# x tile 3 loaded and turned earlier, and filler matmuls on the built-in ones constant, in a fused attention and MLP kernel

## The chip, the cores and the metric

The kernel runs on one core of a Trainium2 chip. The metric is device microseconds of one execution. "Span" is the stretch from the first to the last instruction of a profiled execution; it is about 1.2 us shorter than the time. In the text PE is TensorE, SP the engine that issues most DMAs, and a "turn" is a DMA (DMA_TRANSPOSE in the profile) that writes a 128-row tile transposed. The mean granted clock that the profiles show is 1.00.

## The reference

```
x: [1, 2048, 640] bf16, wqkv [640, 1920], 32 heads of 20
g   = sigmoid(sum(x * gate_w))
q, k, v = split(x @ wqkv);  phi(t) = where(t > 0, t + 1, exp(t)) + 1e-6
a   = linear attention of phi(q), phi(k), v over all tokens, @ wo
x1  = x + shift(gelu(layernorm(x) @ w1)) @ w2
b   = x1 + gelu(layernorm(x1) @ w3) @ w4
out = g * a + (1 - g) * b
```

What matters here is the very start: q and k need x with its features on the partitions, that is, x turned, for all 16 tiles of 128 tokens.

## The kernel before

A small scheduling layer records every operation, works out the waits, and picks the PE order with a time model at build time. The DMA queue of SP carries, in program order, the loads and the turns. PE turns tiles 0 to 2 itself, with a VectorE copy out of PSUM; SP turns tiles 3 to 15.

```python
dma_in(x_tok[:, 0, :], ...); dma_in(x_tok[:, 1, :], ...)      # x tiles 0, 1
load_wq(0)
dma_in(x_tok[:, 2, :], x2[256:384, :], "x2")
for k in range(1, KD):
    load_wq(k)                                                # query weights, 5 slices
for k in range(KD):                                           # key weights, 5 slices
    dma_in(wkg[:, k, 0:D], A_wqkv[128 * k:128 * (k + 1), D:2 * D], "wk%d" % k)
    if k == 2:
        dma_in(x_tok[:, 3, :], x2[384:512, :], "x3")
# ... (gate weight, on the ACT queue)
for c in range(1, NCH):                                       # tiles 4-7, 8-11, 12-15
    dma_in(x_tok[:, 4 * c:4 * c + 4, :], x2[512 * c:512 * (c + 1), :]..., "xc%d" % c)
    for t in range(3 if c == 1 else 4 * c, 4 * c + 4):
        sch.dma("sp", xT[:, :, 128 * t:128 * (t + 1)], x_tok[:, t, :], "trx%d" % (t % 4), transpose=True)
# ...
memset(pool, xn[:, 0, 0:128], 1.0)                            # what the fillers multiply
WARM = 3200; WARM2 = 256
# PE: filler of WARM columns, turn tiles 0 and 1, filler of WARM2, then queries of
# tiles 0-2 slice by slice (with a filler of 256 and the turn of tile 2 in between),
# keys of tiles 0-2, then for t = 3 .. 15: query tile t, key tile t
```

Fillers are matmuls whose result nobody reads. They keep PE busy until data comes.

Of the kernel before, what the change touches and what calls it, by code (L numbers as in the profile page):

```python
# [5 lines left out]
BF16 = mybir.dt.bfloat16  # L6
# [410 lines left out]
def _build(nc, A_x, A_wqkv, A_wo, B_w1, B_w2, B_w3, B_w4, gate_w, out, dbg=None, stop=None):  # L417
    sch = _Sched(nc)
# [41 lines left out]
    ps = nc.alloc_psum_tensor("ps", [128, 8, 512], F32)  # L460
# [18 lines left out]
    x_tok = pa.alloc("x_tok", [128, NT, D], BF16)  # L479
# [9 lines left out]
    xn = pa.alloc("xn", [128, 3, D], BF16)  # L489
# [4 lines left out]
    xT = ra.alloc("xT", [128, KD, S], BF16)  # L494
# [19 lines left out]
    def bank():  # L514
        best = None
        for k_ in range(nbanks[0]):
            b = (bank_rr[0] + k_) % nbanks[0]
            if b in bank_pend or b in bank_hold:
                continue
            lk = sch.locks.get(b)  # L520
            tfree = 0.0 if lk is None else sch.ev_time.get((lk[1].sem, lk[1].val), 1e18)
            if best is None or tfree < best[0]:
                best = (tfree, b)
        bank_rr[0] = best[1] + 1
        bank_pend.add(best[1])
        return best[1]
# [46 lines left out]
    def dve(fn, reads, writes, cost=None):  # L573
        if cost is None:
            n = nfree(writes[0])
            cost = 65.0 + n / 0.96
        return sch.op("dve", fn, reads, writes, cost=cost)
# [7 lines left out]
    def pe(fn, reads, writes, cost=500.0):  # L585
        for w_ in writes:
            sp_, rl = sch.rects(w_)
            if sp_ == "ps":
                for (_p0, _p1, lo, hi) in rl:
                    for b in range(lo // PS_BANK, (hi - 1) // PS_BANK + 1):  # L590
                        bank_pend.discard(b)
        return sch.op("pe", fn, reads, writes, cost=cost)
# [65 lines left out]
    def memset(engf, ap, val):  # L658
        return engf(lambda e: e.memset(ap, val), [], [ap])  # L659
# [13 lines left out]
    def dma_in(out_ap, in_ap, key, **kw):  # L673
        return sch.dma("sp", out_ap, in_ap, key, **kw)
# [11 lines left out]
        load_wq(k)  # L686
    for k in range(KD):
        dma_in(wkg[:, k, 0:D], A_wqkv[128 * k:128 * (k + 1), D:2 * D], "wk%d" % k)
        if k == 2:
            dma_in(x_tok[:, 3, :], x2[384:512, :], "x3")  # L690
    gwr = xn[:, 1, 0:128]
    dve(lambda e: e.memset(gwr, 0.0), [], [gwr])
    sch.dma("act", xn[0:KD, 1, 0:128], gate_w.rearrange("(k p) -> k p", p=128), "gw")
    for c in range(1, NCH):
        dma_in(x_tok[:, 4 * c:4 * c + 4, :], x2[512 * c:512 * (c + 1), :].rearrange("(n p) d -> p n d", p=128), "xc%d" % c)
        for t in range(3 if c == 1 else 4 * c, 4 * c + 4):
            sch.dma("sp", xT[:, :, 128 * t:128 * (t + 1)], x_tok[:, t, :], "trx%d" % (t % 4), transpose=True)

    k_done = {}

# [26 lines left out]
                        wo_rows(h, e, ns), "wo", group_total=5, deps=dp)  # L727
        sch.dma("pool", wo_aug[64:104, 4, :], A_wo[600:D, :], "wo", group_total=5, deps=dp)

    memset(pool, xn[:, 0, 0:128], 1.0)  # L730
    memset(pool, ones_c[:], 1.0)
    memset(pool, wkg[:, :, D:D + 1], 1.0)
    aselect(ident[:], ones_c[:, 0:128], [[-1, 128]], ALU.is_equal, 0, 1)
# [18 lines left out]

    IT = _Items()
    WARM = 3200
    WARM2 = 256

    def t_x(t):
        b = bank()
        tr_group(b, [x_tok[:, t, 128 * k:128 * (k + 1)] for k in range(KD)])
        src = psb(b, 0, D).rearrange("p (k c) -> p k c", k=KD)  # L760
        dst = xT[:, :, 128 * t:128 * (t + 1)]
        if t == 2:
            mm_group(ps[:, b, 448:448 + KD], [(gwr, ident[:, 0:KD])])
        copy(dve, dst, src)
        if t == 2:
            copy(dve, wkg[:, :, D + 1:D + 2], ps[:, b, 448:448 + KD].rearrange("p (k o) -> p k o", o=1))
# [80 lines left out]

    def warmup(cols, cyc):
        b = bank()
        steps = [512] * (cols // 512) + [128] * (cols % 512 // 128)  # L850

        def fn(e):
            ins = None
            for n in steps:
                ins = e.matmul(ps[:, b, 0:n], xn[:, 0, 0:128], xn[:, 0, 0:128].unsqueeze(1).to_broadcast([128, n // 128, 128]), start=True, stop=True)  # L855
            return ins
        pe(fn, [xn[:, 0, 0:128]], [ps[:, b, :]], cost=cols * cyc)

    def q_tile(t):
        tok = slice(128 * t, 128 * (t + 1))  # L860
# [5 lines left out]
    def stream(order, w, n2, done):  # L866
        bs = {}
        for t, k in order:
            if k is None:
                if t is None:  # L870
                    warmup(256, 0.42)
                else:
                    t_x(t)
                continue
            if k == 0:
                bs[t] = pair()
                bank_hold.update((bs[t], bs[t] + 1))
            b = bs[t]
            l = xT[:, k, 128 * t:128 * (t + 1)]

            def fn(e, l=l, b=b, k=k):
                e.matmul(ps[:, b, 0:512], l, w[:, k, 0:512], start=(k == 0), stop=(k == KD - 1))  # L882
                return e.matmul(ps[:, b + 1, 0:n2], l, w[:, k, 512:512 + n2], start=(k == 0), stop=(k == KD - 1))  # L883
            pe(fn, [w[:, k, 0:512 + n2], l], [ps[:, b, 0:512], ps[:, b + 1, 0:n2]], cost=272.0)
            if k == KD - 1:
                bank_hold.difference_update((b, b + 1))
                done(t, b)
# [13 lines left out]
    def addA(name, dur, fn, deps=()):  # L901
        IT.add("A", name, dur, fn, deps)

    addA(("warm",), 0.0, lambda: warmup(WARM, 0.834))
    for i in range(2):
        addA(("tx", i), 0.28, lambda i=i: t_x(i))
    addA(("warm", 1), 0.0, lambda: warmup(WARM2, 0.42))
    addA(("q", 2), 4.08, q_three)
    addA(("k", 1), 2.72, k_two)
# [288 lines left out]
    for t in range(NT):  # L1198
        c = t // 4
# [53 lines left out]
    for t in range(NT):  # L1253
        c = t // 4
# [30 lines left out]
def bass_gated_mix__linear_attn_block__mixer_s_mlp__prompt_kernel(  # L1285
    nc, A_x, A_wqkv, A_wo, B_x, B_w1, B_w2, B_w3, B_w4, gate_w, out
):
    assert tuple(A_x.shape) == (1, S, D) and tuple(out.shape) == (1, S, D)
    assert tuple(A_wqkv.shape) == (D, 3 * D) and tuple(A_wo.shape) == (D, D)
    assert tuple(B_w1.shape) == (D, D) and tuple(B_w2.shape) == (D, D)  # L1290
    assert tuple(B_w3.shape) == (D, F) and tuple(B_w4.shape) == (F, D) and tuple(gate_w.shape) == (D,)
    _build(nc, A_x, A_wqkv, A_wo, B_w1, B_w2, B_w3, B_w4, gate_w, out)
# [28 lines left out]
```

## Time and profile before

| kernel before | us |
|---|---|
| time, median of 3 runs (range) | 260.52 (260.36 to 261.09) |
| span of the profile | 259.8 |
| PE busy | 254.8, 98% of the span |
| first filler matmul starts | 1.05 |
| first query matmul starts | 5.11 |
| query matmul of tile 4, first weight load | 17.50 |

The page of the kernel before: its busy line (engine, us, share, instructions) and the first lines of the chain of work that ended last.

```profile
PE 254.8 (98%) x1655; PEld 133.0 (51%) x1686; DVE 152.0 (59%) x288; ACT 106.5 (41%) x216; POOL 93.6 (36%) x152
...
PE 98%; issue 1%; DVE 0%; POOL 0%; POOLq 0%
```

The whole execution hangs on PE, and PE is never idle for long. So a change of DMA order can gain only where PE waits or works slowly, and that is the start.

The timeline of PE of the kernel before (start us, us, engine, line, operation, tiles, count, and in brackets the idle time before and what ended it):

```profile
1.05 2.85 PE L855 MATMUL ps<-xn 128*128 128x512 bf16 x7 [1.05 <-POOL xn L659]
...
5.11 0.59 PE L882 MATMUL ps<-wq,xT 128*128 128x512 bf16 x1
...
6.95 0.38 PE L882 MATMUL ps<-wq,xT 128*128 128x512 bf16 x1
```

And its weight loads (PEld), around the moment when the array becomes fast, and at tile 4:

```profile
6.88 0.15 PEld L882 LDWEIGHTS ps<-wq,xT 128*128 128x128 bf16 x1
6.95 0.10 PEld L883 LDWEIGHTS ps<-wq,xT 128*128 128x128 bf16 x1
...
17.50 0.10 PEld L600 LDWEIGHTS ps<-wq,xT 128*128 128x128 bf16 x1
```

The fillers wait for a memset of POOL. A weight load takes 0.15 us until 6.88 and 0.10 us from 6.95 on (two loads just after a pause of PE, at 5.08 and 5.11, took 0.10 as well). The 512-column matmuls go from 0.63 to 0.38 us at the same place. That is the speed-up of the array, called "the clock" from here on (a name only); weight loads show it best, because they all have one shape. (The granted clock of the profile reads 1.00 in the slow stretch too; it does not show this.)

SP's timeline of the kernel before, the loads and turns of x (the load that was issued at 7.41 has tiles 4 to 7):

```profile
5.98 0.43 SPq L285 DMA_DIRECT2D x_tok<-in_A_x_dram  x1
...
7.41 0.43 SPq L285 DMA_DIRECT2D x_tok<-in_A_x_dram  x1
...
9.85 1.29 SPq L281 DMA_TRANSPOSE xT<-x_tok  x1
13.54 5.89 SPq L281 DMA_TRANSPOSE xT<-x_tok  x4
19.47 0.58 SPq L285 DMA_DIRECT2D x_tok<-in_A_x_dram  x1
```

A turn that waits for its load is issued as soon as the load has landed: the last landing marks of tile 3 and of tiles 4 to 7 stand at 9.84 and 13.52, the turns at 9.85 and 13.54. When a turned tile has landed is read from its completion marks in the trace, of which there are 16, as many as the DMA engines that the page counts (that each engine sets one is my reading, not shown); the last one counts.

### The profile page before, as it was taken

The numbers are of one execution on the slowest core, as the hardware profiler recorded it, in microseconds if no ns is written. First come the engines' busy times: TensorE is split into PE (matmuls) and PEld (weight loads), VectorE is DVE, ScalarE is ACT, GpSimd is POOL, SyncE is SP. The second block draws the span as 40 slices with busy tenths as digits, with TensorE's granted clock in tenths as the row PEclk, the third lists the DMA queues.
The fourth block names the chain that finished last, engine by engine and source line by source line (L and its number), as shares of the span: only waits on it lengthen the run. The fifth ranks groups of instructions, "written<-read, shape, count | busy, mean of one in ns | idle before, by whom it ended". The sixth has DMA issues, their size and how long they took to land.

```text
span 259.8 us, 4263 instructions
## 1 busy us (share of the span) xinstructions
PE 254.8 (98%) x1655; PEld 133.0 (51%) x1686; DVE 152.0 (59%) x288; ACT 106.5 (41%) x216; POOL 93.6 (36%) x152
## 2 busy tenths in 40 slices
PE   8999999999999999999999999999999999999996
PEld 4555555554445455555444545554455544455453
DVE  1487787899912799999998407993033410143233
ACT  1396767751355766685854140005500045200000
POOL 4003996869963019667904202230011110021001
DMA  6955886581756991552726650132000020000211
GB/s 185 288 86 150 175 207 154 166 140 39 110 113 124 360 327 32 76 101 52 104 46 122 124 73 0 39 83 82 0 3 0 3 101 0 0 3 1 103 50 50
DMA packets 51390, 25.16 MB, mean 97 GB/s; under 512 B 42750, under 2 KB 49959, under 8 KB 51370
## 3 DMA queue, kind: packets, MB, share of 16 engines
q1 hardware_dynamic: 49984, 21.47, 36.0%
q0 software_dynamic: 1136, 3.28, 5.1%
q8 instruction: 13, 0.21, 0.4%
q10 hardware_dynamic: 250, 0.14, 0.2%
q14 instruction: 7, 0.06, 0.1%
HBM read 12.05 MB, written 2.62 MB: 56 GB/s over the span
## 4 chain that ended last, share of the span: by engine, by line
PE 98%; issue 1%; DVE 0%; POOL 0%; POOLq 0%
PE ps L600 61%; PE ps L1160 21%; PE ps L790 8%; PE ps L882 2%; PE ps L855 1%; PE ps L1072 1%; PE ps L1142 1%; PE ps L883 1%; PE ps L611 1%; DVE x_tok L639 0%; PE ps L962 0%; PE ps L991 0%; PE ps L1139 0%; POOL xn L659 0%; POOLq L1306 0%
## 5 line engine op out<-in xcount | busy, mean ns | idle before, releaser
L600 PE MATMUL ps<-xnT,w 128*128 128x512 bf16 x348 | 80.4, 379 | 0.7 <-issue 0.2
L1160 PE MATMUL ps<-w,h2T 128*128 128x512 bf16 (+1 forms) x409 | 58.3, 298 | 0.5 <-issue 0.2
L656 ACT ACTIVATE h2T<-ps 128x512 bf16<-128x512 f32 x52 | 30.5, 598 | 67.6 <-PE ps L600 67.5
L600 PEld LDWEIGHTS ps<-xnT,w 128*128 128x128 bf16 x360 | 34.2, 98 | 38.5 <-issue 0.9
L639 DVE SCALAR_TENSOR_TENSOR x_tok<-ps,stg,abx 128x512 bf16<-128x512 f32 (+1 forms) x32 | 17.3, 550 | 61.5 <-PE ps L1160 61.5
L622 POOL TENSOR_SCALAR abx<-x_tok,stg 128x640 f32<-128x640 bf16 x16 | 15.3, 956 | 99.1 <-DVE x_tok L639 94.9
L1160 PEld LDWEIGHTS ps<-w,h2T 128*128 128x128 bf16 x416 | 32.1, 98 | 24.9 <-issue 1.1
L622 POOL TENSOR_SCALAR xn<-x_tok,st 128x640 bf16<-128x640 bf16 x32 | 34.9, 1099 | 13.8 <-DMA xnT<-xn 13.3
L656 ACT ACTIVATE Er<-ps 128x640 bf16<-128x640 f32 x32 | 22.4, 708 | 17.7 <-PE ps L600 7.9
L655 ACT ACTIVATE junk<-x_tok 128x640 bf16<-128x640 bf16 x32 | 23.7, 739 | 3.1 <-DVE x_tok L637 2.6
L656 ACT ACTIVATE hsT<-ps 128x512 bf16<-128x512 f32 (+1 forms) x32 | 18.9, 593 | 13.1 <-PE ps L600 12.7
L600 PE MATMUL ps<-M_sb,pqnT 128*128 128x128 bf16 (+1 forms) x156 | 23.6, 297 | 0.3
L600 PE MATMUL ps<-w,hsT 128*128 128x512 bf16 (+1 forms) x160 | 23.7, 299 | 0.0
L639 DVE SCALAR_TENSOR_TENSOR abx<-ps,stg,abx 128x640 f32<-128x640 f32 x16 | 14.1, 883 | 12.6 <-PE ps L600 11.6
L600 PE MATMUL ps<-wkg,xT 128*128 128x130 bf16 (+1 forms) x138 | 21.1, 298 | 0.1
L600 PE MATMUL ps<-wq,xT 128*128 128x128 bf16 (+1 forms) x128 | 19.7, 298 | 0.1
L600 PEld LDWEIGHTS ps<-w,hsT 128*128 128x128 bf16 x160 | 13.3, 98 | 12.1
L600 PEld LDWEIGHTS ps<-M_sb,pqnT 128*128 128x128 bf16 x160 | 13.2, 98 | 10.8
L790 PE MATMUL ps<-pk_tok,x_tok 128*128 128x512 bf16 x79 | 17.7, 379 | 0.1
L622 DVE TENSOR_SCALAR Er<-Er 128x640 bf16<-128x640 bf16 x32 | 11.6, 361 | 9.6 <-ACT Er L656 9.3
L1101 DVE TENSOR_TENSOR pq_tok<-pq_tok,dnr 128x300 bf16<-128x300 bf16 (+1 forms) x48 | 16.8, 403 | 0.6
L637 DVE SCALAR_TENSOR_TENSOR x_tok<-ps,x_tok 128x640 bf16<-128x640 f32 x16 | 13.1, 820 | 6.5 <-PE ps L600 5.9
(79 smaller groups left out, 229.1 us busy)
## 6 DMA issues: line engine op xcount, KB each, us to landing
w<-in_B_w_dram SPq DMA_DIRECT2D x1, 2160.0 KB, 9.7
w<-in_B_w_dram SPq DMA_DIRECT2D x1, 2080.0 KB, 15.2
x_tok<-in_A_x_dram SPq DMA_DIRECT2D x3, 640.0 KB, 5.5
out_dram<-x_tok SPq DMA_DIRECT2D x3, 640.0 KB, 3.1
w<-in_B_w_dram POOLq DMA_DIRECT2D x8, 160.0 KB, 3.7
wq<-in_A_wqkv_dram SPq DMA_DIRECT2D x5, 160.0 KB, 3.2
wkg<-in_A_wqkv_dram SPq DMA_DIRECT2D x5, 160.0 KB, 3.9
wv<-in_A_wqkv_dram POOLq DMA_DIRECT2D x1, 800.0 KB, 5.5
```

The source lines that it names most:

```text
L600: ins = e.matmul(out_ap, l, r, start=(i == 0), stop=(i == n - 1))
L611: ins = e.transpose(o, s_, ident[:])
L622: return engf(lambda e: e.tensor_scalar(out_ap, in_ap, s1, s2, op0, op1), rd, [out_ap], cost=cost)
L637: return dve(lambda e: e.scalar_tensor_tensor(out_ap, in0, scalar, in1, op0, op1, accum_out=accum), rd, [out_ap, accum], cost=cost + 70.0)
L639: return dve(lambda e: e.scalar_tensor_tensor(out_ap, in0, scalar, in1, op0, op1), rd, [out_ap], cost=cost)
L655: return act(lambda e: e.activation(out_ap, in_ap, func, bias=bias, scale=scale, accum_out=accum), rd, wr, cost=cost)
L656: return act(lambda e: e.activation(out_ap, in_ap, func, bias=bias, scale=scale), rd, wr, cost=cost)
L790: ins = e.matmul(o, l, r, start=(t0 + q_ == 0), stop=(t0 + q_ == NT - 1))
L855: ins = e.matmul(ps[:, b, 0:n], xn[:, 0, 0:128], xn[:, 0, 0:128].unsqueeze(1).to_broadcast([128, n // 128, 128]), start=True, stop=True)
L882: e.matmul(ps[:, b, 0:512], l, w[:, k, 0:512], start=(k == 0), stop=(k == KD - 1))
L1101: dve(lambda e, o=o, i0=i0, i1=i1: e.tensor_tensor(o, i0, i1, ALU.mult), [i0, dnr[:, 1, sd, :]], [o], cost=cost)
L1160: ins = e.matmul(o, l, r, start=False, stop=(i == KFF - 1), skip_group_check=(n0 > 0))
```

## The change

The intent: get tile 3 turned sooner, by loading it behind the first key slice and issuing its turn ahead of the load of tiles 4 to 7; and start the fillers sooner, by letting them read a constant that the program's preamble has made, in place of a tile that POOL must fill first. The second filler is doubled, which fills what the earlier start frees.

```diff
     for k in range(KD):
         dma_in(wkg[:, k, 0:D], ..., "wk%d" % k)
-        if k == 2:
+        if k == 0:
             dma_in(x_tok[:, 3, :], x2[384:512, :], "x3")
+    def x_turn(t): ...            # the turn of tile t, as before
+    x_turn(3)
     ...
     for c in range(1, NCH):
         dma_in(x_tok[:, 4 * c:4 * c + 4, :], ..., "xc%d" % c)
-        for t in range(3 if c == 1 else 4 * c, 4 * c + 4):
-            sch.dma("sp", xT[...], x_tok[:, t, :], ..., transpose=True)
+        for t in range(4 * c, 4 * c + 4):
+            x_turn(t)
...
-    memset(pool, xn[:, 0, 0:128], 1.0)
-    WARM2 = 256
+    WARM2 = 512
...
+        one = nc.const_aps.tensor(1.0, [128, 512], BF16)
-                ins = e.matmul(ps[:, b, 0:n], xn[:, 0, 0:128], xn[:, 0, 0:128]... repeated, ...)
+                ins = e.matmul(ps[:, b, 0:n], one[:, 0:128], one[:, 0:n], ...)
```

More of the change, by code (lines that the diff above doesn't have):

```diff
@@ L688, in _build, with x_turn @@
         dma_in(wkg[:, k, 0:D], A_wqkv[128 * k:128 * (k + 1), D:2 * D], "wk%d" % k)
-        if k == 2:
+        if k == 0:
             dma_in(x_tok[:, 3, :], x2[384:512, :], "x3")
+    def x_turn(t):
+        sch.dma("sp", xT[:, :, 128 * t:128 * (t + 1)], x_tok[:, t, :], "trx%d" % (t % 4), transpose=True)
+    x_turn(3)
     gwr = xn[:, 1, 0:128]
@@ L695, in _build @@
         dma_in(x_tok[:, 4 * c:4 * c + 4, :], x2[512 * c:512 * (c + 1), :].rearrange("(n p) d -> p n d", p=128), "xc%d" % c)
-        for t in range(3 if c == 1 else 4 * c, 4 * c + 4):
-            sch.dma("sp", xT[:, :, 128 * t:128 * (t + 1)], x_tok[:, t, :], "trx%d" % (t % 4), transpose=True)
+        for t in range(4 * c, 4 * c + 4):
+            x_turn(t)
     k_done = {}
@@ L854, in fn @@
             for n in steps:
-                ins = e.matmul(ps[:, b, 0:n], xn[:, 0, 0:128], xn[:, 0, 0:128].unsqueeze(1).to_broadcast([128, n // 128, 128]), start=True, stop=True)
+                ins = e.matmul(ps[:, b, 0:n], one[:, 0:128], one[:, 0:n], start=True, stop=True)
             return ins
-        pe(fn, [xn[:, 0, 0:128]], [ps[:, b, :]], cost=cols * cyc)
+        pe(fn, [], [ps[:, b, :]], cost=cols * cyc)
     def q_tile(t):
```

## The prediction

> **What bounds the kernel.** The page's busy table has PE at 254.8 us, 98% of the 259.8 us span, and the chain of waits that ended last is PE for 98%. From 13.61 us on the chain has no PE pause over 0.1 us until the tail at 257, so only the first 13.6 us hold anything to win. There (timeline of PE and weight loads) fillers run from 1.05 to about 3.7, the transposes of tiles 0 and 1 to 4.8, two 128-column fillers, then real work from 5.11. The array is slow at first (427 ns per 512 columns in the fillers; 216 ns from 6.95 on). It speeds up between 6.24 and 6.95.
>
> **Fillers.** The first filler waits for the memset of its tile (POOL, 0.79 + 0.20); the built-in ones exist at 0.37, so it can start about 0.2 us earlier, at 0.85. Tile 0 of x lands at 3.29 and tile 1 at 3.62 (landing stamps of the trace), so the transposes can move up by 0.2 us too. The second filler doubles to 512 columns: +0.21 us at the slow clock. Net, the first query matmul (5.11) moves by -0.1 to 0 us. More gain needs the fast clock to come sooner. [...] At best (fast at 5.1) the 1.8 us of slow work shrinks by 0.9 us.
>
> **Tile 3.** Before, x tile 3 was issued at 5.98, landed at 9.84, was turned from 9.85 and the turned tile landed at 14.27, just behind the load of tiles 4-7 (issued 7.41, landed 13.52). It is needed at 14.81: PE did not wait. The change issues it at 5.04, so it should land near 9.0 and be turned by about 12: more slack, nothing gained. The cost follows on the same queue: SP waits for tile 3 (9.0), issues the turn (1.29 us), and only then, at about 10.3 instead of 7.41, issues the load of tiles 4-7. The queue moves 300 GB/s until 12, so the old early issue mostly waited in line; the next chunk, alone, took 4.4 us (19.47 to 23.86). I estimate landing at 14.2 to 15.0, 1 us later than before. Tile 4's turn took 3.9 us before, tile 8's 2.4 us; tile 4 thus lands at 16.8 to 18.8 and is needed at 17.5 (before: 17.45). I expect a PE wait of 0 to 1.2 us before the query matmul of tile 4, mean 0.3. Tiles 5 to 15 keep slack.
>
> **Sum.** About -0.2 (start, clock) + 0.3 (tile 4) - 0.2 for a PE order, chosen by the builder's model, that may shift slightly: nearly nothing. I predict 260.4 us, 8 in 10 between 259.6 and 261.4. Faster by over 2%: 0.01; within 2%: 0.97; slower: 0.02.
>
> **What would show it.** First filler at 0.85; first query matmul at 5.0 to 5.1; the speed-up at 6.2 to 6.9 as before (or earlier: then up to -0.9 us); tile 3's turned landing near 12; the load of tiles 4-7 issued near 10.3; a PE wait on the turn of tile 4 near 17.5; after 20 us only a constant shift.
>
> **What would make it wrong.** [...] the turn of tile 4 taking 4 us again, so that PE loses over 1 us; a builder order that differs in the later stages and leaves gaps.

The sum came to -0.1 us: -0.2, +0.3 and -0.2, from the 260.52 us measured before to 260.4. The start alone was worth -0.1 to 0 us, and the rest of the -0.2 is estimate, not shown.

## The result

| | before | changed |
|---|---|---|
| time, median of 6 runs, us | 260.88 | 261.01 |
| range, us | 260.36 to 261.12 | 260.71 to 261.43 |
| span of the profile, us | 259.81 | 259.76 |

The ratio is 1.0009, with a 95% interval of 0.9995 to 1.0022. A ratio is the mean time of one kernel's fast runs over the mean of the other's fast runs of the same rounds, so it is not quite the ratio of the medians. Nothing that these runs can show has changed. (The median of before went from 260.52 to 260.88 with three more runs: a few tenths of a microsecond is the noise of these numbers.)

The changed kernel's page, the busy line and the chain:

```profile
PE 256.8 (99%) x1685; PEld 133.0 (51%) x1685; DVE 152.4 (59%) x288; ACT 106.6 (41%) x216; POOL 94.2 (36%) x151
...
PE 98%; DVE 1%; issue 0%
```

(The 2 us more of PE busy are matmul records that were missing in the other trace, 1685 against 1655; they aren't work.) Its PE timeline:

```profile
0.83 2.83 PE L860 MATMUL ps<-const-bfloat16-1.0 128*128 128x512 bf16 x7 [0.83 <-PEq L1311]
...
4.95 0.63 PE L887 MATMUL ps<-wq,xT 128*128 128x512 bf16 x1
...
6.82 0.38 PE L887 MATMUL ps<-wq,xT 128*128 128x512 bf16 x1
```

Its weight loads, at the speed-up and at tile 4:

```profile
6.76 0.13 PEld L887 LDWEIGHTS ps<-wq,xT 128*128 128x128 bf16 x1
6.83 0.10 PEld L888 LDWEIGHTS ps<-wq,xT 128*128 128x128 bf16 x1
...
17.47 0.11 PEld L600 LDWEIGHTS ps<-wq,xT 128*128 128x128 bf16 x2
```

And SP's timeline:

```profile
8.69 1.30 SPq L281 DMA_TRANSPOSE xT<-x_tok  x1
10.04 0.57 SPq L285 DMA_DIRECT2D x_tok<-in_A_x_dram  x1
14.22 5.95 SPq L281 DMA_TRANSPOSE xT<-x_tok  x4
20.22 0.59 SPq L285 DMA_DIRECT2D x_tok<-in_A_x_dram  x1
```

Each part did what it was meant to do. The first filler starts 0.22 us sooner. Tile 3 is turned from 8.69 in place of 9.85, and its turned copy lands at 11.34 in place of 14.27. But the load of tiles 4 to 7 now goes out at 10.04 in place of 7.41, and its turns start at 14.22 in place of 13.54.

PE issues the same operations in the same order in both kernels (only the fillers differ), so the two traces can be laid over each other, weight load by weight load. The changed kernel leads by 0.24 us in the fillers, by 0.16 us at the first query weight load (4.92 against 5.08; there it waits for the first query weights, which land at 4.88), by 0.12 us from 5.4 us on, by 0.03 us at the query of tile 4, and by 0.05 us from the next tile to the end. So the lead is lost at one place: the first use of tile 4. Its turned copy landed at 17.43 us, and the weight load started at 17.47.

### The profile page after: what moved, and what is told of

Its sections match the earlier page's. It is cut to its first block, busy times and chain, and to the rows that moved or that the text cites. A ratio compares the mean times of both kernels' runs of the same rounds, so it can differ in the third digit from the quotient of the medians.

```text
span 259.8 us, 4291 instructions
## 1 busy us (share of the span) xinstructions
PE 256.8 (99%) x1685; PEld 133.0 (51%) x1685; DVE 152.4 (59%) x288; ACT 106.6 (41%) x216; POOL 94.2 (36%) x151
## 4 chain that ended last, share of the span: by engine, by line
PE 98%; DVE 1%; issue 0%
PE ps L600 61%; PE ps L1165 22%; PE ps L794 8%; PE ps L887 2%; PE ps L860 1%; PE ps L1077 1%; PE ps L1147 1%; PE ps L611 1%; PE ps L888 1%; DVE x_tok L639 0%; PE ps L967 0%; PE ps L996 0%; DVE xT L665 0%; PE ps L1144 0%
## 5 line engine op out<-in xcount | busy, mean ns | idle before, releaser
L600 PE MATMUL ps<-xnT,w 128*128 128x512 bf16 x360 | 81.5, 379 | 0.0
L656 ACT ACTIVATE Er<-ps 128x640 bf16<-128x640 f32 x32 | 22.4, 707 | 17.6 <-PE ps L600 8.5
L600 PE MATMUL ps<-M_sb,pqnT 128*128 128x512 bf16 (+1 forms) x160 | 24.3, 299 | 0.0
L600 PE MATMUL ps<-wq,xT 128*128 128x512 bf16 (+1 forms) x130 | 19.8, 299 | 0.0
L1106 DVE TENSOR_TENSOR pq_tok<-pq_tok,dnr 128x300 bf16<-128x300 bf16 (+1 forms) x48 | 16.8, 404 | 0.6
```

The source lines that it names most:

```text
L600: ins = e.matmul(out_ap, l, r, start=(i == 0), stop=(i == n - 1))
L656: return act(lambda e: e.activation(out_ap, in_ap, func, bias=bias, scale=scale), rd, wr, cost=cost)
L1106: dve(lambda e, o=o, i0=i0, i1=i1: e.tensor_tensor(o, i0, i1, ALU.mult), [i0, dnr[:, 1, sd, :]], [o], cost=cost)
```

## The experiments

Two theories came out of this comparison. Theory A: tile 4's turn is late because of something that hits it in both kernels, a 16 KB DMA packet of the queue that the page calls "instruction". In the kernel before, the first of them runs from 15.36 to 16.35 us, in the changed kernel from 14.66 to 15.78. Rival B: the later load of tiles 4 to 7 is what costs, as the prediction had it. The clock was a question of its own: does the speed-up come at a fixed time, a fixed time after the first matmul, or at random?

The packets' line in the DMA view of the kernel before (queue, kind: packets, MB, share of 16 engines):

```profile
q8 instruction: 13, 0.21, 0.4%
```

All profiles in one table, from the traces. "First filler" is the first weight load of the first filler (in e4_no_first_filler, which has none, of the transposes). "Fast" is the interval between the start of the last slow weight load and that of the first fast one (loads of 0.10 us just after a pause of PE are left out). "Tile 3" and "tile 4" are the landings of their turned copies. "q4" is the first weight load of the query matmul of tile 4.

| run | first filler | fast | tile 3 | tile 4 | q4 | span | span minus q4 |
|---|---|---|---|---|---|---|---|
| before | 1.05 | 6.88-6.95 | 14.27 | 17.45 | 17.50 | 259.81 | 242.31 |
| changed | 0.80 | 6.76-6.83 | 11.34 | 17.43 | 17.47 | 259.76 | 242.29 |
| e1_fillers | 0.80 | 4.41-5.33 | 14.29 | 16.61 | 17.01 | 259.34 | 242.33 |
| e2_tile3 | 1.05 | 6.24-6.41 | 11.70 | 17.61 | 17.65 | 259.94 | 242.29 |
| e3_pieces | 0.80 | 3.88-4.06 | 11.61 | 18.49 | 18.53 | 261.61 | 243.08 |
| e4_no_first_filler | (3.29) | 8.95-9.28 | 11.53 | 18.69 | 18.73 | 261.02 | 242.29 |
| e5_tile4 | 0.80 | 3.56-3.74 | 12.07 | 12.87 | 16.65 | 258.98 | 242.33 |
| e6_order | 0.80 | 3.67-3.76 | 11.83 | 12.70 | 16.65 | 258.98 | 242.33 |
| e7_ahead | 0.80 | 4.41-6.05 | 12.07 | 12.79 | 17.10 | 259.44 | 242.33 |
| e8_after_again | 0.80 | 4.31-4.39 | 11.78 | 17.13 | 17.17 | 259.45 | 242.28 |
| e9_old_fillers | 1.05 | 4.12-4.22 | 12.00 | 13.09 | 16.82 | 259.15 | 242.33 |
| e10_order_again | 0.80 | 3.77-3.87 | 12.03 | 12.98 | 16.68 | 259.02 | 242.35 |

Two readings are worth the whole table. The last column is constant to 0.07 us in all but one run: the start of tile 4's query decides the span. And in all five profiles with tile 3 early and tile 4 in the bulk load (changed, e2, e3, e4 and e8, with another clock each time) q4 is the landing of tile 4 plus 0.04 us: PE was waiting for it. The same holds for the kernel before (17.45 and 17.50): there tile 4 landed just as PE came to it, so even the kernel before had next to no slack at tile 4, although no wait shows.

### e1_fillers: the fillers alone

```diff
 (kernel before, with the filler part of the change; tile 3 as before)
-    memset(pool, xn[:, 0, 0:128], 1.0)
-    WARM2 = 256
+    WARM2 = 512
+        one = nc.const_aps.tensor(1.0, [128, 512], BF16)     # and the fillers read it
```

> Fillers of the change alone (built-in ones, 512 columns), tile 3 as before. Matching weight loads of this trace against the kernel before: in the changed kernel they stood 0.12 us earlier from the first query matmul to 17.5 us and only 0.03 us earlier from the query matmul of tile 4 on. Theory A [...]: here too 0.12 us earlier up to 17.4, tile 4's turn landing at 17.3 to 17.5 with one straggler, and only 0.0 to 0.06 us earlier after it. Rival B (the later load of tiles 4-7 is what costs): tile 4 in time, 0.12 us earlier to the end. Time against before, either way: ratio 0.999 to 1.001.

Measured: ratio 0.9988 (0.9975 to 1.0001). The profile didn't answer the question as put, because the clock came at about 5 us in it and not at 6.8: PE led by 0.82 us at 8 us and not by 0.12. It answered another. The lead fell to 0.43 us at the query of tile 3. The weight loads of e1_fillers there:

```profile
14.33 0.11 PEld L600 LDWEIGHTS ps<-wq,xT 128*128 128x128 bf16 x2 [0.25 <-DMA xT<-x_tok]
```

In the old order, an early clock makes PE wait for tile 3, whose turned copy lands at 14.29 behind the load of tiles 4 to 7. So tile 3's move is not for nothing; the one profile of before, with its late clock, hid that. Tile 4 landed at 16.61, before PE came to it.

### e2_tile3: tile 3's move alone

```diff
 (kernel before, with the tile 3 part of the change; fillers as before)
-        if k == 2:
+        if k == 0:
             dma_in(x_tok[:, 3, :], x2[384:512, :], "x3")
+    x_turn(3)                    # ahead of the load of tiles 4-7
```

> Tile 3's move alone, fillers as before. Both: no shift of PE before 17.5 us, tile 3's turned tile landing near 11.5 instead of 14.27. Theory A: tile 4's turn issued near 14.2 and landing at 17.2 to 17.6 [...], PE shift afterwards 0 to 0.1 us later. Rival B: the turn itself, begun 0.7 us later, lands 0.7 us later than before (18.1), PE shift 0.6 us later. Time: A ratio 0.999 to 1.001, B 1.002.

Measured: ratio 0.9996 (0.9973 to 1.0019). Tile 3's copy landed at 11.70 as both expected; the clock came 0.5 us earlier than in before, so PE led by 0.29 us until it met tile 4. The weight loads of e2_tile3:

```profile
17.65 0.11 PEld L600 LDWEIGHTS ps<-wq,xT 128*128 128x128 bf16 x2 [0.42 <-DMA xT<-x_tok]
```

PE waited 0.42 us and left 0.15 us behind the kernel before. The landing, 17.61, is within A's 17.2 to 17.6 to the rounding and not B's 18.1; the shift of 0.15 us is between the two. The turn began 1.2 us later than in before (14.73 against 13.54) and still landed only 0.15 us later: the kernel before lost over a microsecond in its turn, and B alone has no reason for that.

### e3_pieces: more, smaller filler matmuls

```diff
 (changed kernel)
-        steps = [512] * (cols // 512) + [128] * (cols % 512 // 128)
+        steps = [128] * (cols // 128)
```

> The changed kernel with its fillers cut into 128-column matmuls (25 and 4 in place of 7 and 1): same columns, same time at the slow clock, but 42 more PE instructions ahead of the real work[...]. Theory A: the issue of tile 4's turn takes 1.3 us instead of 2.0, its 16 completion stamps stand within 0.3 us and the last lands at 16.5 to 17.1; PE keeps its 0.12 us lead on the kernel before to the end. Rival B: tile 4 lands at 17.4 again and the lead falls to 0.03. Time: no difference that rounds can show, ratio 0.998 to 1.001.

The clause cut above put the packet ahead of tile 4's turn, near 12.2 us and 2.5 us sooner than in the changed kernel, for the 42 PE instructions more; the reading of the packets that it rested on was not shown.

Measured: ratio 1.0023 (0.9998 to 1.0048), and that estimate was a miss in its size: the packet came at 13.88, 0.8 us sooner than in the changed kernel and not 2.5, in time with the load of tiles 4 to 7 and not with the turn. These are the completion marks of that load in e3_pieces (us):

```
14.30 14.35 14.37 14.38 14.41 14.42 14.47 14.49 14.50 14.56 14.57 14.59 14.61 14.63 14.68 16.04
```

Fifteen of the 16 marks stand by 14.68; the last came 1.36 us later. The marks of tile 4's turn in the kernel before have the same form: fifteen from 15.78 to 15.94, the last at 17.45, with the packet at 15.36. In e3_pieces the turn, begun at 16.05 with no packet in its way, took 2.44 us with all marks within 0.2 us. So what was late moved when the packet moved, which supports A; A's promise that PE would keep its lead failed, because the delay stood in the load instead. PE waited for tile 4, and, in this profile alone, for tiles 13 and 14 as well (weight loads of e3_pieces; the third line is tile 14):

```profile
18.53 0.11 PEld L600 LDWEIGHTS ps<-wq,xT 128*128 128x128 bf16 x2 [1.57 <-DMA xT<-x_tok]
...
46.57 0.11 PEld L600 LDWEIGHTS ps<-wq,xT 128*128 128x128 bf16 x2 [0.72 <-DMA xT<-x_tok]
...
49.61 0.11 PEld L600 LDWEIGHTS ps<-wq,xT 128*128 128x128 bf16 x2 [0.20 <-DMA xT<-x_tok]
```

Over the profiles, tile 4's turn took 2.43 to 2.44 us where the packet was over before the turn was issued (e3) or within 0.7 us of it (e8), and 2.9 to 4.3 us in the other five, where the packet ended 1.3 to 2.8 us after the issue (before 3.9, changed 3.2, e1 3.1, e2 2.9, e4 4.3). The five later profiles, where tile 5's turn is the first behind the bulk load, agree: 2.38 to 2.41 us where the packet ended 0.1 to 0.9 us after the issue (e9, e5, e10, e7), and 2.60 us where it ended 1.03 us after (e6). So over twelve profiles the turn's delay goes with the end of the packet. How the packet would do it is not one picture, though: of the turns, only that of the kernel before has one late mark of 16. In changed, e1, e2 and e4 all 16 marks stand within 0.22 us, so there the whole turn is late and not one mark of it; that part stays open.

The packets took 0.9 to 1.6 us each. The trace of the kernel before has 13 of them. In it, 186 PE instructions start before the first packet and 3216 before the last, 252 from one packet to the next on average (207 to 289); the changed kernel has 179 and 3251, 256 on average (201 to 298). PE has 3341 matmuls and weight loads on the page of the kernel before, any other compute engine 288 instructions at most. That the packets have to do with PE's instructions is estimate from these counts; what they carry no trace shows. Nor does the trace tell which DMA engine a packet ran on, or in what order an engine worked, so that a packet holds up the DMA beside it is inferred from the timing, not shown.

### e4_no_first_filler: when does the clock come?

```diff
 (changed kernel)
-    addA(("warm",), 0.0, lambda: warmup(WARM, 0.834))
```

> The changed kernel without its first filler (3200 columns); PE idles until tile 0 lands at 3.3 us. Three theories of when the array's fast clock comes (6.8 us in both kernels so far, weight loads going from 150 to 98 ns). [...] still 6.8, the filler is worth nothing, PE shift 0 and time ratio 0.999 to 1.001. Count of about 6 us from the first matmul: speed-up near 9.3, about 1.2 us lost. [...]

(Of the three theories, the first is a fixed time and the third a time that varies by run.)

Measured: ratio 1.0012 (0.9985 to 1.0038). The weight loads of e4_no_first_filler:

```profile
8.95 0.15 PEld L888 LDWEIGHTS ps<-wq,xT 128*128 128x128 bf16 x1
9.28 0.10 PEld L887 LDWEIGHTS ps<-wq,xT 128*128 128x128 bf16 x1 [0.18 <-issue]
...
18.73 0.11 PEld L600 LDWEIGHTS ps<-wq,xT 128*128 128x128 bf16 x2 [0.41 <-DMA xT<-x_tok]
```

The fixed time is out: without the filler the clock came 2.2 to 2.5 us later than in the changed kernel, and in e1, e2 and e3 sooner. A count of 6 us from the first matmul fits this run, but not e1, e3, e5, e6, e8 or e10, where the same fillers led to the fast clock at 3.6 to 5.3 us. Over the twelve profiles the speed-up comes 2.8 to 6.0 us after the first PE work, a width of 3.2 us; in five of them (e3, e5, e6, e9 and e10) it came after 2.8 to 3.3 us. What decides the moment no run here shows. One program shows much of the spread: changed 6.8 and e8_after_again 4.3 us. (A difference between chips is not excluded for this pair; e1 to e4 ran on one chip and, as four programs, spread from 3.1 to 6.0 us after the first PE work.)

### e5_tile4: take away the wait on tile 4

```diff
 (changed kernel)
-        if k == 0:
-            dma_in(x_tok[:, 3, :], x2[384:512, :], "x3")
+        if k < 2:
+            dma_in(x_tok[:, 3 + k, :], x2[384 + 128 * k:512 + 128 * k, :], "x%d" % (3 + k))
     x_turn(3)
+    x_turn(4)
     # the first bulk load has tiles 5-7; their turns follow as before
```

> The changed kernel, with x tile 4 loaded alone right behind tile 3 and turned right behind it; the bulk load then has tiles 5-7. Theory A, as it stands after four runs: the clock's speed-up comes at a random moment (5.1 to 6.9 us with fillers, by run), and an early one is worth nothing in the changed kernel because PE then waits for tile 4's turn (landing 17.4 to 18.7 in all traces of the new order). Here tile 4's turned copy should land near 13.5, PE never wait at that place, and the lead that PE has at 13 us last to 40 us. On average over runs 0.3 to 0.8 us faster than before: ratio 0.997 to 0.999, with a spread of runs of over 1 us that follows the clock. Rival (what sets the time is downstream, the gain is absorbed later): lead at 13 us but no shorter span, ratio 0.9995 to 1.0005.

(The table has the speed-up of the profiles by then, with fillers, from 3.9 us on, in e3_pieces, and not from 5.1.)

Measured: ratio 0.9986 (0.9971 to 1.0001). Tile 4's copy landed at 12.87, PE didn't wait for it, and the lead of 0.82 us that PE had at 13 us was still there in the span (258.98 against 259.81). The rival, a lead absorbed downstream, is out for this profile: nothing after tile 4 takes it back. In the measured times the gain is small: the interval just reaches 1. The weight loads of e5_tile4 at tile 4, with no idle before:

```profile
16.54 0.15 PEld L600 LDWEIGHTS ps<-wkg,xT 128*128 128x128 bf16 x2
16.65 0.10 PEld L600 LDWEIGHTS ps<-wq,xT 128*128 128x128 bf16 x1
```

### e6_order and e10_order_again: the query order on top

```diff
 (e5_tile4; (tile, slice) of the first queries)
-        order = [..., (0, 1), (1, 1), (2, 0), (0, 2), (1, 2), ...]
+        order = [..., (0, 1), (1, 1), (0, 2), (2, 0), (1, 2), ...]
```

> As e5_tile4, and the query matmul of tile 0 slice 2 goes ahead of that of tile 2 slice 0, which waits for a VectorE copy (0.21 us of PE idle in before and after). Expected: that idle gone when weight slice 2 is there (it landed at 6.3 to 6.8), so 0 to 0.25 us less than e5_tile4; ratio to before 0.996 to 0.999. If it is lost downstream, same as e5_tile4.

Measured: ratio 0.9971 (0.9959 to 0.9983). This is the first version that is clear of the noise against the kernel before: 260.28 us median against 261.01 of the same rounds, and its five runs, 260.13 to 260.59, lie below all but the lowest of the six of the changed kernel in the same rounds (260.55 to 261.73). But against e5_tile4 the profile shows no gain, the same span of 258.98: with the early clock of both profiles PE waits for the query weights (1.2 us in e5_tile4 and 1.3 us in e6_order, by the waits of the weight loads) instead of the VectorE copy (0.4 us in the kernel before, none listed in these two). The transposes of tile 2 on PE are faster too with that clock (the program calls transpose; the trace lists these as MATMUL): five took 0.44 us in e6_order, from 5.53, and 0.74 us in the slow stretch of the kernel before, from 6.34. SP's timeline of e6_order, with both turns ahead of the bulk load:

```profile
8.79 2.63 SPq L281 DMA_TRANSPOSE xT<-x_tok  x2
11.47 0.58 SPq L285 DMA_DIRECT2D x_tok<-in_A_x_dram  x1
15.13 4.13 SPq L281 DMA_TRANSPOSE xT<-x_tok  x3
```

Its weight loads at tile 4 read as those of e5_tile4, at the same 16.65 us.

> e6_order again, beside e9 on one chip, to see whether it beats the kernel before a second time: ratio 0.996 to 0.9985 if the gain is real, 0.999 to 1.001 if the first interval was luck. PE does not wait for tile 4; span 258.9 to 259.7 [...].

Measured again: ratio 0.9978 (0.9953 to 1.0003), median 260.54 against 261.00. The size is the same; this interval just reaches 1, because the runs of before spread from 260.26 to 262.47. One later wait shows in its profile, on tile 12, which landed 0.04 us before its use (weight loads of e10_order_again):

```profile
41.22 0.11 PEld L600 LDWEIGHTS ps<-wq,xT 128*128 128x128 bf16 x2 [0.18 <-DMA xT<-x_tok]
```

About 0.12 us of that idle time stands at this point in the other profiles too, where tile 12 had landed earlier; the last column of the table grew by 0.02 us at most.

### e7_ahead: later loads out sooner

```diff
 (e6_order; in place of the loop over c; x_load(t0, t1) loads tiles t0 to t1 - 1)
+    x_load(5, 8)
+    for t in range(5, NT):
+        x_turn(t)
+        if t in (6, 10):
+            x_load(t + 2, t + 6)      # the next four tiles, before the last turn of these
```

> As e6_order, and the loads of tiles 8-11 and 12-15 go out one turn earlier, between the turns of the chunk before, so that the chain load, four turns, load on the one queue (10.3 to 10.8 us a chunk against 12 us of PE work) has more slack. If no tile after 4 is waited for, same time as e6_order within 0.1%; if runs are sometimes held by tiles 8 to 15 (one trace of e3_pieces shows PE waiting 0.6 and 0.2 us for tiles 13 and 14), up to 0.3 us less on average.

Measured: ratio 0.9977 (0.9965 to 0.9989), against 0.9971 of e6_order: no gain, as expected if no later tile is waited for. Its profile has no wait on a turned tile, and more slack: tiles 12 and 14 landed 3.9 and 8.4 us before their use, in e6_order 0.7 us each.

### e8_after_again: the changed kernel a second time

> The changed kernel once more, on the same chip as the three runs above, to compare with them directly and for another look at the clock. [...] tile 4's turned copy lands at 17.4 to 18.7 and query matmul of tile 4 starts with it (within 0.1 us) if the clock came early. [...] Ratio to before 0.998 to 1.002.

Measured: ratio 0.9993 (0.9978 to 1.0008). The clock came at 4.3 us, 2.4 us sooner than in the first profile of the same kernel. PE then stood before tile 4 (weight loads of e8_after_again, around the speed-up and at tile 4; the first line is two loads, the later from 4.31):

```profile
4.20 0.23 PEld L611 LDWEIGHTS ps<-ident,x_tok 128*128 128x128 bf16 x2
4.39 0.10 PEld L860 LDWEIGHTS ps<-const-bfloat16-1.0 128*128 128x128 bf16 x1
...
17.17 0.55 PEld L600 LDWEIGHTS ps<-wq,xT 128*128 128x128 bf16 x4 [0.27 <-DMA xT<-x_tok]
```

The mean of its six runs is 260.91 us, that of e6_order's five of the same rounds 260.33: freeing tile 4, with the query order, is worth 0.58 us. (One run of e8_after_again, 261.73, makes 0.16 of it. e5_tile4, with tile 4 alone, has a mean of 260.65 in the same rounds, 0.26 us below e8_after_again, so how the 0.58 us divides between tile 4 and the query order is not settled.)

### e9_old_fillers: the better order with the old fillers

```diff
 (e6_order)
+    memset(pool, xn[:, 0, 0:128], 1.0)      # fillers read this tile again
-    WARM2 = 512
+    WARM2 = 256
```

> e6_order with the fillers of the kernel before (a memset tile, 256 columns), so tile 3 and tile 4 early and the query order, but not the earlier first filler. If e6's gain (ratio 0.9971, 95% 0.9959 to 0.9983) comes from freeing PE of the wait on tile 4: ratio 0.996 to 0.9985 here too. If the earlier fillers make it (0.24 us earlier start, sooner fast clock): 0.9985 to 1.0005. The clock's speed-up again at a random time, 4.0 to 7.1 us, with first filler at 1.05.

(The 4.0 to 7.1 us are about what a first filler at 1.05 gives with the 2.8 to 6.0 us from first PE work to fast clock of the profiles before this one.)

Measured: ratio 0.9999 (0.9968 to 1.003). Four of its six runs lie from 260.40 to 260.72, like e6_order's; two lie at 261.53 and 261.96. Its profile is one of the good ones (q4 at 16.82, span 259.15). What share the earlier fillers have in e6's gain stays open: the ratio itself lies in the range that the expectation gave to the fillers, the interval holds both answers, and I have no profile of the two long runs.

## Why the prediction was right

The time, 261.01 us, is in the range of 259.6 to 261.4, and "within 2%" was right. That alone says little: the range is 1.8 us wide, six times the largest term of the sum. What was tested is the trade: a small gain at the start, lost again in a wait on tile 4. Against the sum of -0.2, +0.3 and -0.2 us, the first pair of profiles has -0.12 us before tile 4, +0.11 us of wait there and 0 for the order. That the total was near is in part luck, because one of its terms did not exist. Point by point:

- What bounds the kernel: right. The span is the start of tile 4's query plus 242.3 us in eleven of twelve profiles, so nothing after it matters.
- First filler at 0.85: 0.80. First query matmul 0 to 0.1 us earlier: 0.16 us, a little more, and then held by the first query weights (landed 4.88).
- The clock: right that it may come earlier; e8 and the changed kernel, which are one program, differ by 2.4 us. What sets its moment no run here shows. "At best 0.9 us" was about right too: e5 and e6, with the earliest clocks, reach q4 0.85 us before the kernel before. What the prediction missed is that the changed kernel cannot use it, because PE stands at tile 4 whatever the clock does.
- Load of tiles 4 to 7 issued near 10.3 and landed at 14.2 to 15.0: 10.04 and 14.21 in the profile, 14.68 in e8. Tile 4 at 16.8 to 18.8: 17.43 and 17.13. PE wait 0 to 1.2 us, mean 0.3: 0.11 us in the first profile (from the query of tile 3 to that of tile 4 it took 2.83 us; where tile 4 is early, in e5, e6, e7, e9 and e10, it takes 2.72) and 0.27 us in e8. Right.
- "More slack, nothing gained" from tile 3: wrong in part. It was read from one profile with a late clock. With an early clock the old order makes PE wait 0.25 us for tile 3 (e1). So the change trades a wait on tile 3 for a wait on tile 4, and that is why nothing is left of it.
- The term of -0.2 us for another PE order: there was none. The order of every compute engine is the same but for the fillers and the memset. This term should have been 0.
- "Tiles 5 to 15 keep slack": so in both profiles of the changed kernel (at least 2.2 and 1.25 us from landing to use). Not in e3_pieces, where tiles 13 and 14 were waited for, nor in e10_order_again, where tile 12 landed 0.04 us before its use.

The reason given for tile 4's long turn was none at all ("took 3.9 us before"); the runs put it down, as far as timing can tell, to a 16 KB packet of the "instruction" queue. So theory A and rival B are both part of the answer, by an estimate from the traces. In the first profile of the changed kernel an undisturbed turn (2.43 us, from e8) issued at 14.22 would have landed at 16.65, and PE came to tile 4 at about 17.36: the later load alone would have cost nothing, and the wait of 0.11 us there is the packet's. In e8 the turn took its undisturbed 2.43 us, and PE, early because of the clock, still waited 0.27 us: there the later load alone is the cause, as the prediction had it.

## What to carry to other kernels

Where a queue serves a consumer in order, moving one transfer forward moves the next ones back (here tile 3's turn went out 1.16 us sooner and the load of tiles 4 to 7 2.63 us later): look for the next item that the consumer needs and see how much slack it has, before counting a gain. Read a wait from several profiles when something random, like the moment when the array speeds up (2.8 to 6.0 us after the first PE work here), decides who comes first: one profile of the kernel before showed neither tile as waited for. The remedy here was small, one more tile loaded alone and turned early. With another query order it gave 0.2 to 0.3% in two measurements, of which one is clear of the noise; alone it gave 0.14% with an interval that reaches 0, and with the old fillers nothing that could be measured.
